# Reordering the opening loads, the first group's loads and the last stores of a fused attention and gated-unit kernel

## The chip, the cores and the metric

The kernel runs on one core of one Trainium2 chip. The metric is device time in microseconds (us), the median over runs; "span" is the time that a profile covers, 1.7 to 1.9 us less than the run's time.

TensorE is called PE in the profile, VectorE DVE, ScalarE ACT, GpSimd POOL, and SyncE, which here only issues DMAs, SP. "PEld" is the loading of weights into TensorE.

## The reference

```python
# x: 1 x 2048 x 640; 32 heads of 192; keys and values: the last W = 512 of 2048 positions
xn = layernorm(x)
s  = attention(xn @ wq, k_cache[last 512], v_cache[last 512]) @ wo      # softmax(q k^T / sqrt(192)) v
h  = sigmoid(xn @ w_gate) * (xn @ w_up)                                # 640 -> 1536
g  = silu(h @ w_down)                                                  # 1536 -> 640
out = x + s * g
```

## The kernel before

The kernel first computes the gate `g` for all 16 row tiles (4 blocks of 512 rows), then the attention in 8 groups of 4 heads, each over the 4 row blocks. Three places matter here.

The opening. Row tile 0 is normalised, transposed on TensorE (`turn_pe`), and used at once, while weights and further tiles still arrive. Two weight loads are issued by ScalarE, all else by SyncE:

```python
def turn_pe(t):
    pT = ...                                             # one PSUM bank
    for c in range(NCD):
        nc.tensor.transpose(pT[:, c, :], ln[t][:, c * P:(c + 1) * P], ident[:])
    nc.scalar.activation(xnT[:, 0, 3:NCD, r], pT[:, 3:NCD, :], AF.Copy)   # two copies out,
    nc.vector.tensor_copy(xnT[:, 0, 0:3, r], pT[:, 0:3, :])               # one after the other

load_f(nc.scalar, wg_sb, wg_r, 0, 2)      # column blocks 0 and 1 of w_gate: rows of 512 bytes, 320 KB
load_f(nc.scalar, wu_sb, wu_r, 0, 2)      # the same of w_up
load_x(0, 1)                              # row tiles, 160 KB each, on SyncE
load_x(1, 1)
load_x(2, 2)
for f0, f1 in ((2, 4), (4, 8), (8, NF)):
    load_f(nc.sync, wg_sb, wg_r, f0, f1)
    load_f(nc.sync, wu_sb, wu_r, f0, f1)
...
piece(0, 0, lambda: normal(1))            # piece(t, f): tile t, column block f, 2 x 5 matmuls
piece(0, 1, first_half(2), 1)             # with turn_pe(1) in front
piece(1, 0, second_half(2))
piece(1, 1)
piece(0, 2, lambda: normal(2))
...                                       # 16 pieces in all, then matmuls over all 512 rows
```

The middle. Further blocks are transposed by DMA from SyncE (`turn_dma`, `xnT<-xn`). Behind the third block's loop GpSimd issues the loads of the first head group, 2.5 MB:

```python
def load_group(g):                        # wq, keys, values: nc.gpsimd.dma_start(...) throughout
...
if b == 2:
    load_group(0)
```

The tail. `u` numbers the units of group and block; `turn_out` transposes the attention output by DMA (`oT<-o_st`) and `project` multiplies by `wo`, gates, adds and stores. In the last unit the transposes come in halves, the stores go to ScalarE's queue, one add runs on GpSimd, and the last row tile is cut in three:

```python
for h, k in enumerate((2, 0, 1, 3)):
    values(u, h, k)
    if h % 2:
        turn_out(u, 3 * (h // 2), 3 * (h // 2) + 3)          # 4 half transposes, twice, on SyncE
for q, k in ((1, 2), (2, 0), (3, 1)):
    project(u - 1, q, k, nc.scalar)
for q, k in ((0, 3), (1, 2), (2, 0)):
    project(u, q, k, nc.scalar, None, nc.gpsimd if q == 2 else None)
project(u, 3, (1, 3, 2), None, ((0, 256), (256, 512), (512, D)))
# in project: r_sb = fin.tile([P, D], BF16, name="row")      # a ring of 4 buffers
```

The softmax here doesn't subtract the row's maximum and nothing guards it: scores larger than these inputs give would overflow.

Of the kernel before, what the change touches and what calls it, by code (L numbers as in the profile page):

```python
# [8 lines left out]
AF = mybir.ActivationFunctionType  # L9
# [6 lines left out]
def kernel(  # L16
# [76 lines left out]
    def load_group(g):  # L93

        d = grp.setdefault(g, {})
        d["wq"] = load2.tile([P, NCD, GW], BF16, name="wq_sb")
        nc.gpsimd.dma_start(d["wq"][:], wq_r[:, :, g * GW:(g + 1) * GW])
        kst = load1.tile([P, 4, KC, DH], BF16, name="k_st")
        kv = slice(Sk - W, Sk)
        nc.gpsimd.dma_start(  # L100
            kst[:].rearrange("p h j d -> p h (j d)"),
            A_k_cache[0, 4 * g:4 * g + 4, kv, :].rearrange("h (p j) d -> p h (j d)", j=KC),
        )
        d["v"] = vbuf[g % 2]
        for h in range(4):
            nc.gpsimd.dma_start(  # L106
                d["v"][:, h, :, 0:DH],
                A_v_cache[0, 4 * g + h, kv, :].rearrange("(p j) d -> p j d", j=KC),
            )
        kp = load1.tile([P, 2, KC, DJ, P], BF16, name="k_perm")  # L110
        for h in range(4):
            nc.gpsimd.tensor_copy(
                kp[:, h // 2, :, :, (h % 2) * H2:(h % 2) * H2 + H2],
                kst[:, h, :, :].rearrange("p c (i j) -> p c j i", j=DJ),
            )
        d["kp"] = kp
# [17 lines left out]
    with ExitStack() as bctx:  # L134
# [11 lines left out]
        def load_x(t, n):  # L146

            x = xpool.tile([P, n, D], BF16, name=f"x_sb{n}", bufs=1 if n == 2 else 2)
            nc.sync.dma_start(x[:], xf[t * P:(t + n) * P, :].rearrange("(q p) d -> p q d", p=P))
            for i in range(n):  # L150
                xt[t + i] = x[:, i, :]
# [5 lines left out]
        load_f(nc.scalar, wg_sb, wg_r, 0, 2)  # L157
        load_f(nc.scalar, wu_sb, wu_r, 0, 2)
        load_x(0, 1)
        load_x(1, 1)  # L160
        load_x(2, 2)
        for f0, f1 in ((2, 4), (4, 8), (8, NF)):
            load_f(nc.sync, wg_sb, wg_r, f0, f1)
            load_f(nc.sync, wu_sb, wu_r, f0, f1)
# [42 lines left out]
        def turn_pe(t):  # L207

            pT = bank[3][:, t % 2, 0:NCD * H2].bitcast(BF16).rearrange("p (c n) -> p c n", c=NCD)
            for c in range(NCD):  # L210
                nc.tensor.transpose(pT[:, c, :], ln[t][:, c * P:(c + 1) * P], ident[:])
            r = slice(t * P, (t + 1) * P)
            nc.scalar.activation(xnT[:, 0, 3:NCD, r], pT[:, 3:NCD, :], AF.Copy)
            nc.vector.tensor_copy(xnT[:, 0, 0:3, r], pT[:, 0:3, :])
# [7 lines left out]
        def gated(b, f, r0, r1, k, between=None):  # L222
            if b not in hT:
                hT[b] = hpool.tile([P, NF, TB], BF16, name="hT")
            for half, w in ((0, wg_sb), (1, wu_sb)):
                for c in range(NCD):
                    nc.tensor.matmul(bank[k][:, half, 0:r1 - r0], lhsT=w[:, c, f * P:(f + 1) * P],  # L227
                                     rhs=xnT[:, b, c, r0:r1], start=(c == 0), stop=(c == NCD - 1))
            sig = bwork.tile([P, TB], BF16, name="sig")
# [31 lines left out]
        dummy(19)  # L261
# [8 lines left out]
        stats_end(1)  # L270
        k = 0

        def piece(t, f, before=None, turn=None):
            nonlocal k
            if turn is not None:
                turn_pe(turn)
            gated(0, f, t * P, (t + 1) * P, k, before)
            k = (k + 1) % 3

        def first_half(t):  # L280
            return lambda: stats_half(t, 0)
# [5 lines left out]
        piece(0, 1, first_half(2), 1)  # L287
        piece(1, 0, second_half(2))
        piece(1, 1)
        piece(0, 2, lambda: normal(2))  # L290
        piece(0, 3, first_half(3))
        piece(1, 2, second_half(3))
        piece(1, 3, None, 2)
        piece(2, 0, lambda: normal(3))
        piece(2, 1)
        piece(2, 2)
        piece(2, 3, None, 3)
# [6 lines left out]
        for b in range(1, NB):  # L304
# [11 lines left out]
            if b == 2:  # L316
                load_group(0)
# [89 lines left out]
    def turn_out(u, c0=0, c1=GC):  # L407
        if u not in oT:
            oT[u] = oT_pool.tile([P, GC, TB], BF16, name="oT")
        for q in range(TQ):  # L410
            nc.sync.dma_start_transpose(oT[u][:, c0:c1, q * P:(q + 1) * P],  # L411
                                        o_st[u][:, q, c0 * P:c1 * P])

    def project(u, q, k, out_eng=None, parts=None, add_eng=None):
# [3 lines left out]
        last = g == NG - 1  # L418
        split = ((0, 512), (512, D))
        if parts is None:  # L420
            for cc in range(GC):
                for d0, d1 in split:
                    nc.tensor.matmul(wide(k)[:, d0:d1], lhsT=oT[u][:, cc, q * P:(q + 1) * P],  # L423
                                     rhs=wo[:, cc, d0:d1], start=(cc == 0), stop=(cc == GC - 1))
            if last:
                o_sb = fin.tile([P, D], F32, name="o_sb", bufs=2)
                r_sb = fin.tile([P, D], BF16, name="row")
                nc.vector.tensor_tensor(o_sb[:], wide(k)[:, 0:D], gate[:, t, :], ALU.mult)  # L428
                (add_eng or nc.vector).tensor_tensor(r_sb[:], o_sb[:], acc[:, t, :], ALU.add)  # L429
                out_eng.dma_start(of[t * P:(t + 1) * P, :], r_sb[:])  # L430
            elif g == 0:
                nc.vector.tensor_copy(acc[:, t, :], wide(k)[:, 0:D])
            else:
                nc.vector.tensor_tensor(acc[:, t, :], wide(k)[:, 0:D], acc[:, t, :], ALU.add)  # L434
        else:

            o_sb = fin.tile([P, D], F32, name="o_sb", bufs=2)
            r_sb = fin.tile([P, D], BF16, name="row")
            for i, (d0, d1) in enumerate(parts):
                ps = wide(k[i])[:, 0:d1 - d0]  # L440
                for cc in range(GC):
                    nc.tensor.matmul(ps, lhsT=oT[u][:, cc, q * P:(q + 1) * P],
                                     rhs=wo[:, cc, d0:d1], start=(cc == 0), stop=(cc == GC - 1))
                nc.vector.tensor_tensor(o_sb[:, d0:d1], ps, gate[:, t, d0:d1], ALU.mult)
                nc.vector.tensor_tensor(r_sb[:, d0:d1], o_sb[:, d0:d1], acc[:, t, d0:d1], ALU.add)  # L445
                eng = (nc.scalar, nc.sync)[i % 2]
                eng.dma_start(of[t * P:(t + 1) * P, d0:d1], r_sb[:, d0:d1])
        if g == NG - 2:
# [5 lines left out]
    for u in range(NU):  # L454
# [8 lines left out]
        if b == 1 and g + 1 < NG:  # L463
            load_group(g + 1)
# [19 lines left out]
    for h, k in enumerate((2, 0, 1, 3)):  # L484
        values(u, h, k)
        if h % 2:
            turn_out(u, 3 * (h // 2), 3 * (h // 2) + 3)
    for q, k in ((1, 2), (2, 0), (3, 1)):
        project(u - 1, q, k, nc.scalar)
    for q, k in ((0, 3), (1, 2), (2, 0)):  # L490
        project(u, q, k, nc.scalar, None, nc.gpsimd if q == 2 else None)
    project(u, 3, (1, 3, 2), None, ((0, 256), (256, 512), (512, D)))
# [30 lines left out]
```

## Time and profile before

| | before |
|---|---|
| time, median (range of its first 3 runs) | 940.91 us (940.86 to 941.36) |
| span of the profile | 939.5 us |
| TensorE busy | 919.6 us (98%) |
| first real matmul / first dense 512-column matmul | 7.12 / 21.19 us |
| last values matmuls begin | 914.38 us |
| last VectorE instruction ends | 936.27 us |

Lines of the profile's page, before: the span; the busy time of each engine, with its share of the span and its instructions; and the chain of work that ended last, by engine.

```profile
span 939.5 us, 18100 instructions
...
PE 919.6 (98%) x7962; PEld 548.1 (58%) x8042; DVE 471.0 (50%) x754; ACT 305.8 (33%) x342; POOL 132.5 (14%) x161
...
PE 95%; DMA 2%; DVE 1%; issue 1%; ACT 0%; SPq 0%; POOL 0%; DVEq 0%
```

TensorE does nearly all of the work and is nearly all of the chain. So its idle time is what can be won. The list of waits of TensorE over the whole span, before; each line reads who waited, on what line, for whom, then the total in us, the number of waits and the longest:

```profile
engine line waited for: us in total, times, longest us
PE bank L227 <- DMA xnT<-xn: 3.4, 1, 3.4
PE bank L423 <- DMA oT<-o_st: 2.2, 2, 1.7
PE bank L227 <- DVE xnT L214: 1.6, 3, 0.7
PE bank L211 <- DVE xn L203: 1.5, 2, 1.3
PE bank L177 <- DVE eps_t L168: 1.2, 1, 1.2
```

These are waits at the edges. The first is one wait in the middle, at 116 us, for the DMA transposes of the last activation block; the second lies in the tail; the third and fourth in the opening (the fifth is the start itself). From 172 to 900 us there is next to none.

Stretches of the opening, before (start and end in us; busy us and instructions of each engine; then the granted TensorE clock, the DMA share and GB/s):

```profile
core 0: us, PE busy (x) PEld busy (x) DVE busy (x) ACT busy (x) POOL busy (x), PEclk, DMA share, GB/s
5.20:8.60 3.40, 1.71 (x20) 1.13 (x18) 1.90 (x7) 1.75 (x4) 0.57 (x1) 1.00 1.16 311
8.60:12.00 3.40, 2.91 (x28) 2.91 (x29) 2.13 (x7) 0.68 (x3) 0.00 (x0) 0.51 1.10 344
```

In the second stretch TensorE is busy, but at half of its clock (0.51): groups of five 128-column matmuls follow each other every 0.53 us there, and every 0.28 us from 12.2 us on. Ahead of it lies a stretch with 1.71 us of work in 3.4.

The transposes of activations (`xnT`), 95 to 125 us, before: the four issues (duration of an issue in ns, first and last start), who made TensorE idle and for how long, and the time from issue to landing:

```profile
L218 SPq DMA_TRANSPOSE xnT<-xn x4: 1200/1202/1202, 102.9 to 110.1; - x4
...
  DMA xnT<-xn: 3.4, 1
...
DMA to landing us min/median/max: 2.6/2.6/9.3
```

Three land in 2.6 us, one in 9.3. In this time GpSimd's 2.5 MB arrive.

The end of the chain of work that ended last, before (start, duration, what):

```profile
924.94 1.27 SPq L411
...
926.26 4.90 DMA oT<-o_st
...
931.21 1.00 PE bank L423 x6
...
932.23 0.04 DVE o_sb L428
...
933.42 1.53 DVE row L445
...
935.98 0.29 DVE row L445
```

SyncE is still issuing transposes at 926.2 us, one of them lands 4.9 us later, TensorE goes on at 931.21, and VectorE closes. Its add of 256 columns at 933.42 us takes 1.53 us while an add of GpSimd's runs (933.14 to 934.68 us); its next one of that size takes 0.42.

### The profile page before, as it was taken

What the parts mean: (1) busy time and instruction counts of PE and PEld (TensorE: products, weight loads), DVE (VectorE), ACT (ScalarE), POOL (GpSimd) and SP (SyncE); (2) the same over time, 40 slices, a digit from 0 to 9 for tenths busy, and PEclk for the clock granted to TensorE, in tenths of its full rate; (3) what the DMA queues carried; (4) which work ended last, traced back from release to release, by engine and by line L of the source; (5) the groups of instructions that cost most, each with busy time, mean ns of one, the idle gap of its engine ahead of it and who ended that gap; (6) DMA issues with size and microseconds to landing.
All of it is one profiled execution on the core that took longest, in us unless ns stands there. A gap on an engine that the chain in (4) does not pass through costs nothing.

```text
span 939.5 us, 18100 instructions
## 1 busy us (share of the span) xinstructions
PE 919.6 (98%) x7962; PEld 548.1 (58%) x8042; DVE 471.0 (50%) x754; ACT 305.8 (33%) x342; POOL 132.5 (14%) x161
## 2 busy tenths in 40 slices
PE   8999999999999999999999999999999999999996
PEld 6445444466666666666666666666666666666664
DVE  5553523355555555555555555555555555555657
ACT  3222212343333333333333333333333333333340
POOL 1000210300020002000200020002000205555000
PEclk9999999999999999999999999999999999999999
DMA  9300330424423343424343433273325343422323
GB/s 310 84 19 11 96 76 1 154 74 81 101 65 76 65 114 68 76 56 123 68 77 56 122 68 77 54 124 68 77 51 127 69 79 70 87 67 58 63 67 86
DMA packets 156767, 76.69 MB, mean 82 GB/s; under 512 B 139024, under 2 KB 150032, under 8 KB 156688
## 3 DMA queue, kind: packets, MB, share of 16 engines
q1 hardware_dynamic: 146288, 42.86, 23.5%
q0 software_dynamic: 7936, 30.94, 11.9%
q10 hardware_dynamic: 2464, 1.74, 0.7%
q8 instruction: 63, 1.03, 0.5%
q14 instruction: 16, 0.13, 0.1%
HBM read 39.45 MB, written 2.62 MB: 45 GB/s over the span
## 4 chain that ended last, share of the span: by engine, by line
PE 95%; DMA 2%; DVE 1%; issue 1%; ACT 0%; SPq 0%; POOL 0%; DVEq 0%
PE bank L381 21%; PE bank L423 21%; PE bank L398 18%; PE bank L363 18%; PE bank L227 10%; PE bank L239 6%; DMA xnT<-xn 1%; PE bank L331 1%; DMA oT<-o_st 1%; DMA x_sb<-in_A_x_dram 0%; DVE row L445 0%; DVE st L185 0%; DVE row L429 0%; DVE o_sb L428 0%; SPq L411 0%
## 5 line engine op out<-in xcount | busy, mean ns | idle before, releaser
L367 ACT ACTIVATE E<-bank 128x1024 bf16<-128x1024 f32 x256 | 257.8, 1023 | 477.5 <-PE bank L363 465.5
L381 PE MATMUL bank<-xnT,wq_sb 64*128 64x512 bf16 x1860 | 231.4, 376 | 0.0
L423 PE MATMUL bank<-wo_sb,oT 128*128 128x512 bf16 (+1 forms) x1461 | 224.0, 296 | 5.5 <-DMA oT<-o_st 2.2
L363 PE MATMUL bank<-qT,kT 64*128 64x512 bf16 x1536 | 202.2, 377 | 0.2 <-DVE o_st L404 0.2
L398 PE MATMUL bank<-vbuf,E 128*128 128x193 bf16 x2048 | 191.0, 247 | 0.0
L398 PEld LDWEIGHTS <-E 128*128 128x128 bf16 x2048 | 167.8, 98 | 24.2 <-issue 13.6
L388 DVE CAST qT<-bank 128x1024 bf16<-128x1024 f32 x93 | 113.9, 1225 | 132.8 <-PE bank L381 132.8
L423 PEld LDWEIGHTS <-oT 128*128 128x128 bf16 x1524 | 120.1, 98 | 78.8 <-DMA oT<-o_st 2.8
L381 PEld LDWEIGHTS <-wq_sb 64*128 64x128 bf16 x1860 | 97.3, 100 | 104.5
L363 PEld LDWEIGHTS <-kT 64*128 64x128 bf16 x1536 | 73.3, 94 | 90.0 <-issue 8.9
L404 DVE TENSOR_TENSOR o_st<-bank,rden 128x768 bf16<-128x768 f32 x128 | 122.6, 958 | 4.6 <-DVE rden L403 0.2
L434 DVE TENSOR_TENSOR acc<-bank,acc 128x640 f32<-128x640 f32 x96 | 79.2, 825 | 43.7 <-PE bank L423 43.7
L227 PE MATMUL bank<-xnT,wg_sb 128*128 128x512 bf16 (+1 forms) x296 | 62.1, 340 | 5.2 <-DMA xnT<-xn 3.4
L227 PE MATMUL bank<-xnT,wu_sb 128*128 128x512 bf16 (+1 forms) x295 | 62.1, 339 | 0.3
L386 DVE COPY seen<-bank 128x2 f32<-128x2 f32 x93 | 14.8, 160 | 94.1 <-PE bank L381 93.9
L233 DVE TENSOR_TENSOR hT<-bank,sig 128x512 bf16<-128x512 f32 (+1 forms) x60 | 35.0, 583 | 51.1 <-ACT sig L230 51.1
L403 DVE RECIPROCAL rden<-bank 128x4 f32<-128x4 f32 x128 | 23.4, 182 | 71.3 <-PE bank L398 71.2
L230 ACT ACTIVATE sig<-bank 128x512 bf16<-128x512 f32 (+1 forms) x60 | 30.7, 512 | 79.7 <-PE bank L227 76.6
L239 PE MATMUL bank<-wd_sb,hT 128*128 128x128 bf16 (+1 forms) x376 | 52.4, 298 | 0.4
L106 POOL DMA_DIRECT2D vbuf<-in_A_v_cache_dram x32 | 23.9, 747 | 183.7 <-PE bank L398 183.7
L227 PEld LDWEIGHTS <-wg_sb 128*128 128x128 bf16 x300 | 27.2, 100 | 31.1 <-issue 5.9
L239 PEld LDWEIGHTS <-hT 128*128 128x128 bf16 x384 | 29.6, 98 | 23.2
(49 smaller groups left out, 264.9 us busy)
## 6 DMA issues: line engine op xcount, KB each, us to landing
wq_sb<-in_A_wq_dram POOLq DMA_DIRECT2D x8, 960.0 KB, 6.8
wo_sb<-in_A_wo_dram POOLq DMA_DIRECT2D x8, 960.0 KB, 7.1
k_st<-in_A_k_cache_dram POOLq DMA_DIRECT2D x8, 768.0 KB, 8.7
vbuf<-in_A_v_cache_dram POOLq DMA_DIRECT2D x32, 192.0 KB, 3.0
row<-in_A_x_dram POOLq DMA_DIRECT2D x16, 160.0 KB, 2.7
oT<-o_st SPq DMA_TRANSPOSE x132, 2.6
x_sb<-in_A_x_dram SPq DMA_DIRECT2D x3, 640.0 KB, 10.8
wd_sb<-in_B_w_down_dram SPq DMA_DIRECT2D x1, 1920.0 KB, 14.0
```

Source lines behind the costliest of these rows:

```text
L227: nc.tensor.matmul(bank[k][:, half, 0:r1 - r0], lhsT=w[:, c, f * P:(f + 1) * P], rhs=xnT[:, b, c, r0:r1], start=(c == 0), stop=(c == NCD - 1))
L230: nc.scalar.activation(sig[:, 0:r1 - r0], bank[k][:, 0, 0:r1 - r0], AF.Sigmoid)
L233: nc.vector.tensor_tensor(hT[b][:, f, r0:r1], bank[k][:, 1, 0:r1 - r0], sig[:, 0:r1 - r0], ALU.mult)
L239: nc.tensor.matmul(wide(k)[:, d0:d1], lhsT=hT[b][:, f, q * P:(q + 1) * P], rhs=wd_sb[:, f, d0:d1], start=(f == 0), stop=(f == NF - 1))
L363: nc.tensor.matmul(bank[k][:, i, :], lhsT=kT[r, pr, j, c * P:(c + 1) * P], rhs=q[r, pr * DJ + j, :], start=(j == 0), stop=(j == DJ - 1))
L367: nc.scalar.activation(E[u, pr][:, c, :, :], bank[k][:], AF.Exp, scale=scale_qk)
L381: nc.tensor.matmul(bank[k][:, half, :], lhsT=wq[r, c, col:col + DJ * (P - 1) + 1:DJ], rhs=xnT[r, b, c, :], start=(c == 0 and not second), ...
L388: nc.vector.tensor_copy(qT[u][:, 2 * m:2 * m + 2, :], bank[k][:])
L398: nc.tensor.matmul(o4[:, q, 0:DH + 1], lhsT=e[:, c, h % 2, q * P:(q + 1) * P], rhs=v[:, h, c, 0:DH + 1], start=(c == 0), stop=(c == KC - 1))
L404: nc.vector.tensor_tensor(o_st[u][:, :, h * DH:(h + 1) * DH], o4[:, :, 0:DH], rden[:].to_broadcast([P, TQ, DH]), ALU.mult)
L423: nc.tensor.matmul(wide(k)[:, d0:d1], lhsT=oT[u][:, cc, q * P:(q + 1) * P], rhs=wo[:, cc, d0:d1], start=(cc == 0), stop=(cc == GC - 1))
L434: nc.vector.tensor_tensor(acc[:, t, :], wide(k)[:, 0:D], acc[:, t, :], ALU.add)
```

## The change

The intent: put the opening loads on one queue in the order in which they are needed; copy each opening transpose out of PSUM with one engine; run four pieces of tile 0 before tile 1 is needed and put the transposes inside a piece; load the first head group behind the transposes on SyncE's own queue; and in the tail transpose whole, with the stores of the last-but-one unit queued behind the transposes. Two small companions are not shown: one more warm-up matmul at the start (20 for 19) and four single-tile buffers for the row tiles of the opening.

```diff
-    def load_group(g):
+    def load_group(g, eng):
-        nc.gpsimd.dma_start(d["wq"][:], wq_r[:, :, g * GW:(g + 1) * GW])
+        eng.dma_start(d["wq"][:], wq_r[:, :, g * GW:(g + 1) * GW])
 ...                                                   (keys and values likewise)
-        load_f(nc.scalar, wg_sb, wg_r, 0, 2)
-        load_f(nc.scalar, wu_sb, wu_r, 0, 2)
         load_x(0, 1)
+        load_f(nc.sync, wg_sb, wg_r, 0, 2)
         load_x(1, 1)
-        load_x(2, 2)
-        for f0, f1 in ((2, 4), (4, 8), (8, NF)):
+        load_f(nc.sync, wu_sb, wu_r, 0, 2)
+        load_x(2, 1)
+        load_f(nc.sync, wg_sb, wg_r, 2, 4)
+        load_f(nc.sync, wu_sb, wu_r, 2, 4)
+        load_x(3, 1)
+        for f0, f1 in ((4, 8), (8, NF)):
 ...
-            nc.scalar.activation(xnT[:, 0, 3:NCD, r], pT[:, 3:NCD, :], AF.Copy)
-            nc.vector.tensor_copy(xnT[:, 0, 0:3, r], pT[:, 0:3, :])
+            if t == 0:
+                nc.vector.tensor_copy(dst, pT)
+            else:
+                nc.scalar.activation(dst, pT, AF.Copy)
 ...                               (gated() gets amid: turn_pe between its gate and its up matmuls)
-        piece(0, 1, first_half(2), 1)
-        piece(1, 0, second_half(2))
-        piece(1, 1)
-        piece(0, 2, lambda: normal(2))
-        piece(0, 3, first_half(3))
-        piece(1, 2, second_half(3))
-        piece(1, 3, None, 2)
+        piece(0, 1)
+        piece(0, 2, second_half(2), 1)
+        piece(0, 3)
+        piece(1, 0, lambda: normal(2))
+        piece(1, 1, lambda: stats_half(3, 0))
+        piece(1, 2, second_half(3), 2)
+        piece(1, 3)
 ...
-                load_group(0)
+                load_group(0, nc.sync)
 ...
     for h, k in enumerate((2, 0, 1, 3)):
         values(u, h, k)
-        if h % 2:
-            turn_out(u, 3 * (h // 2), 3 * (h // 2) + 3)
+    turn_out(u)
     for q, k in ((1, 2), (2, 0), (3, 1)):
-        project(u - 1, q, k, nc.scalar)
+        project(u - 1, q, k, nc.sync)
     for q, k in ((0, 3), (1, 2), (2, 0)):
-        project(u, q, k, nc.scalar, None, nc.gpsimd if q == 2 else None)
-    project(u, 3, (1, 3, 2), None, ((0, 256), (256, 512), (512, D)))
+        project(u, q, k, nc.scalar)
+    project(u, 3, 1, None)                 # one product, two adds and two stores (384 and 256 columns)
```

More of the change, by code (lines that the diff above doesn't have):

```diff
@@ L91 @@
     grp = {}
-    def load_group(g):
+    def load_group(g, eng):
         d = grp.setdefault(g, {})
         d["wq"] = load2.tile([P, NCD, GW], BF16, name="wq_sb")
-        nc.gpsimd.dma_start(d["wq"][:], wq_r[:, :, g * GW:(g + 1) * GW])
+        eng.dma_start(d["wq"][:], wq_r[:, :, g * GW:(g + 1) * GW])
         kst = load1.tile([P, 4, KC, DH], BF16, name="k_st")
         kv = slice(Sk - W, Sk)
-        nc.gpsimd.dma_start(
+        eng.dma_start(
             kst[:].rearrange("p h j d -> p h (j d)"),
@@ L105, in load_group @@
         for h in range(4):
-            nc.gpsimd.dma_start(
+            eng.dma_start(
                 d["v"][:, h, :, 0:DH],
@@ L146, in load_x @@
         def load_x(t, n):
-            x = xpool.tile([P, n, D], BF16, name=f"x_sb{n}", bufs=1 if n == 2 else 2)
+            x = xpool.tile([P, n, D], BF16, name=f"x_sb{n}", bufs=4 if n == 1 else 2)
             nc.sync.dma_start(x[:], xf[t * P:(t + n) * P, :].rearrange("(q p) d -> p q d", p=P))
@@ L211, in turn_pe @@
                 nc.tensor.transpose(pT[:, c, :], ln[t][:, c * P:(c + 1) * P], ident[:])
-            r = slice(t * P, (t + 1) * P)
-            nc.scalar.activation(xnT[:, 0, 3:NCD, r], pT[:, 3:NCD, :], AF.Copy)
-            nc.vector.tensor_copy(xnT[:, 0, 0:3, r], pT[:, 0:3, :])
+            dst = xnT[:, 0, :, t * P:(t + 1) * P]
+            if t == 0:
+                nc.vector.tensor_copy(dst, pT)
+            else:
+                nc.scalar.activation(dst, pT, AF.Copy)
         def turn_dma(t):
@@ L220, with gated @@
         hT = {}
-        def gated(b, f, r0, r1, k, between=None):
+        def gated(b, f, r0, r1, k, between=None, amid=None):
             if b not in hT:
@@ L228, in gated @@
                                      rhs=xnT[:, b, c, r0:r1], start=(c == 0), stop=(c == NCD - 1))
+                if half == 0 and amid is not None:
+                    turn_pe(amid)
             sig = bwork.tile([P, TB], BF16, name="sig")
@@ L258, in norm_piece @@
             return step if i <= TQ else None
-        dummy(19)
+        dummy(20)
         stats_half(0, 0)
@@ L270, with piece @@
         stats_end(1)
+        stats_half(2, 0)
         k = 0
-        def piece(t, f, before=None, turn=None):
+        def piece(t, f, before=None, amid=None):
             nonlocal k
-            if turn is not None:
-                turn_pe(turn)
-            gated(0, f, t * P, (t + 1) * P, k, before)
+            gated(0, f, t * P, (t + 1) * P, k, before, amid)
             k = (k + 1) % 3
-        def first_half(t):
-            return lambda: stats_half(t, 0)
         def second_half(t):
@@ L286 @@
         piece(0, 0, lambda: normal(1))
-        piece(0, 1, first_half(2), 1)
-        piece(1, 0, second_half(2))
-        piece(1, 1)
-        piece(0, 2, lambda: normal(2))
-        piece(0, 3, first_half(3))
-        piece(1, 2, second_half(3))
-        piece(1, 3, None, 2)
+        piece(0, 1)
[5 more added lines that the diff above has]
+        piece(1, 3)
         piece(2, 0, lambda: normal(3))
         piece(2, 1)
-        piece(2, 2)
-        piece(2, 3, None, 3)
+        piece(2, 2, None, 3)
+        piece(2, 3)
         for f in range(4):
@@ L405, in values, with turn_out, project @@
                                 rden[:].to_broadcast([P, TQ, DH]), ALU.mult)
-    def turn_out(u, c0=0, c1=GC):
-        if u not in oT:
-            oT[u] = oT_pool.tile([P, GC, TB], BF16, name="oT")
+    def turn_out(u):
+        oT[u] = oT_pool.tile([P, GC, TB], BF16, name="oT")
         for q in range(TQ):
-            nc.sync.dma_start_transpose(oT[u][:, c0:c1, q * P:(q + 1) * P],
-                                        o_st[u][:, q, c0 * P:c1 * P])
-    def project(u, q, k, out_eng=None, parts=None, add_eng=None):
+            nc.sync.dma_start_transpose(oT[u][:, :, q * P:(q + 1) * P], o_st[u][:, q, :])
+    def project(u, q, k, out_eng):
         g, b = u // NB, u % NB
@@ L417, in project @@
         t = b * TQ + q
-        last = g == NG - 1
-        split = ((0, 512), (512, D))
-        if parts is None:
-            for cc in range(GC):
-                for d0, d1 in split:
-                    nc.tensor.matmul(wide(k)[:, d0:d1], lhsT=oT[u][:, cc, q * P:(q + 1) * P],
-                                     rhs=wo[:, cc, d0:d1], start=(cc == 0), stop=(cc == GC - 1))
-            if last:
-                o_sb = fin.tile([P, D], F32, name="o_sb", bufs=2)
-                r_sb = fin.tile([P, D], BF16, name="row")
-                nc.vector.tensor_tensor(o_sb[:], wide(k)[:, 0:D], gate[:, t, :], ALU.mult)
-                (add_eng or nc.vector).tensor_tensor(r_sb[:], o_sb[:], acc[:, t, :], ALU.add)
-                out_eng.dma_start(of[t * P:(t + 1) * P, :], r_sb[:])
-            elif g == 0:
-                nc.vector.tensor_copy(acc[:, t, :], wide(k)[:, 0:D])
-            else:
-                nc.vector.tensor_tensor(acc[:, t, :], wide(k)[:, 0:D], acc[:, t, :], ALU.add)
-        else:
+        for cc in range(GC):
+            for d0, d1 in ((0, 512), (512, D)):
+                nc.tensor.matmul(wide(k)[:, d0:d1], lhsT=oT[u][:, cc, q * P:(q + 1) * P],
+                                 rhs=wo[:, cc, d0:d1], start=(cc == 0), stop=(cc == GC - 1))
@@ L437, in project @@
+        if g == NG - 1:
             o_sb = fin.tile([P, D], F32, name="o_sb", bufs=2)
             r_sb = fin.tile([P, D], BF16, name="row")
+            nc.vector.tensor_tensor(o_sb[:], wide(k)[:, 0:D], gate[:, t, :], ALU.mult)
+            parts = ((0, D),) if out_eng is not None else ((0, 384), (384, D))
             for i, (d0, d1) in enumerate(parts):
-                ps = wide(k[i])[:, 0:d1 - d0]
-                for cc in range(GC):
-                    nc.tensor.matmul(ps, lhsT=oT[u][:, cc, q * P:(q + 1) * P],
-                                     rhs=wo[:, cc, d0:d1], start=(cc == 0), stop=(cc == GC - 1))
@@ L444, in project @@
-                nc.vector.tensor_tensor(o_sb[:, d0:d1], ps, gate[:, t, d0:d1], ALU.mult)
                 nc.vector.tensor_tensor(r_sb[:, d0:d1], o_sb[:, d0:d1], acc[:, t, d0:d1], ALU.add)
-                eng = (nc.scalar, nc.sync)[i % 2]
+                eng = out_eng or (nc.scalar, nc.sync)[i]
                 eng.dma_start(of[t * P:(t + 1) * P, d0:d1], r_sb[:, d0:d1])
+        elif g == 0:
+            nc.vector.tensor_copy(acc[:, t, :], wide(k)[:, 0:D])
+        else:
+            nc.vector.tensor_tensor(acc[:, t, :], wide(k)[:, 0:D], acc[:, t, :], ALU.add)
@@ L463 @@
         if b == 1 and g + 1 < NG:
-            load_group(g + 1)
+            load_group(g + 1, nc.gpsimd)
             load_wo(g + 1)
```

## The prediction

> **What bounds the kernel.** TensorE. The page's busy table has it busy 919.6 of 939.5 us, and the chain of waits puts 95% of the span on its matmuls. The list of waits shows hardly any from 172 to 900 us. So only three places can give time.
>
> 1. Opening. In the timeline the dense 512-column matmuls start at 21.19 us. The first real matmul starts at 7.12 us; 16 pieces of ten 128-column matmuls (0.56 us each at full rate) and three transposes (0.28 us each) need 9.8 us, but took 14.07. It waits 1.25 us for the second normalised tile, 1.6 for transposed copies. From about 8.8 to 12.2 us the stretches view shows a granted clock of 0.52: 31 matmuls took 3.1 us where full rate gives 1.74. The Trainium skill ("TensorE: Matmul & The Clock Gate", Part 1) says a mostly idle window of about 3.4 us halves the clock; the trace agrees: one halved window of 3.4 us, after a window with 1.7 us of work.
> 2. Middle, at 116 us: TensorE idles 3.35 us for the last transpose of the last activation block. That one took 9.3 us to land, its siblings 2.6; GpSimd's 2.5 MB for the first head group moves beside it (303 GB/s at 116 to 120 us).
> 3. Tail. After the last values (919.9 us) TensorE waits 0.5 and 1.7 us for transposes; the last took 4.9 us to land against a median of 2.5, beside output stores from the other queue. Each transpose, whole or half, costs 1.25 us to issue; there are eight halves. The last matmul ends at 933.84, VectorE at 936.27 (one add took 1.53 us beside GpSimd's), the span at 939.5.
>
> **The change, costed.**
> 1. The first tile is alone at the head of the queue: lands about 2.8 us instead of 3.41. ScalarE loses two issues (1 us). The first transposed copy, 0.62 us on VectorE alone, no longer waits for ScalarE's table load. First real matmul about 6.2. Four pieces of tile 0 run before tile 1 is needed, and transposes sit inside pieces. The opening bytes move at about 340 GB/s as before, so the third piece may wait some 0.5 us for weights and for tile 1's normalisation (about 8.2 us). TensorE does about 2.4 us of work in the window that before had 1.7, so I expect no halved clock (60%). Dense matmuls from about 17.1: gain 4 us; 2.5 if the halved window returns.
> 2. First-group loads go on the transposes' own queue, behind them: the last lands in about 2.6 us, before it is needed. Gain 3.35.
> 3. Four whole transposes from about 921.2 us, issued by 926.3, no stores beside them: landings about 923.7, 925.0, 926.2, 927.5. TensorE runs through to about 931.1. VectorE (seven times 1.68 us from 921.5) then is the limit, ending about 933.3 instead of 936.3. Gain 2.9.
>
> All three are critical, one after another, so they add: 10.2 us. **Predicted 930.8 us, 80% range 928.6 to 933.4.** Faster by over 2% (under 922): 1%; within 2%: 98.5%; slower: 0.5%.
>
> **Right or wrong shows in:** first real matmul near 6.2 us, first 512-column matmul near 17, no clock of 0.5 there; no idle of TensorE before the last activation block and transposes all landing in about 2.6 us; no TensorE wait for transposes in the tail, last VectorE instruction about 3.2 us before the end.
>
> **What would make it wrong:** weights landing later behind the tiles on one queue, and the idle time halving the clock again; VectorE stuck behind the third tile's statistics; a block of loads still slowing the transpose ahead of it; row buffers held up by stores queued behind the transposes.

## The result, and the profile after

The changed kernel takes 932.92 us (median of 4 runs, 932.66 to 933.39) against 941.13 us (4 runs, 940.86 to 942.36) of the kernel before in the same rounds. The ratio is 0.9911, with a 95% interval of 0.9894 to 0.9928: 8.2 us less, within 2%. A ratio here is the mean time of one kernel's fast runs over that of the other's of the same rounds, so not quite the ratio of the medians quoted.

Lines of the profile's page, after:

```profile
span 931.5 us, 18073 instructions
...
PE 917.8 (99%) x7957; PEld 546.1 (59%) x8037; DVE 469.3 (50%) x749; ACT 306.2 (33%) x341; POOL 126.5 (14%) x154
...
PE 97%; DMA 1%; DVE 1%; issue 1%; SPq 0%; DVEq 0%
```

The waits of TensorE, after (line 231 is line 227 of before):

```profile
engine line waited for: us in total, times, longest us
PE bank L231 <- DMA wg_sb<-in_B_w_gate_dram: 1.4, 1, 1.4
PE bank L180 <- DVE eps_t L171: 1.2, 1, 1.2
PE bank L231 <- DMA wu_sb<-in_B_w_up_dram: 0.6, 2, 0.4
PE bank L231 <- DVE xnT L216: 0.3, 1, 0.3
```

The waits for transposes by DMA are gone, in the middle and in the tail. New are waits for weights in the opening: 1.4 us for a gate block (`wg_sb`) and 0.6 us, in two waits, for up blocks (`wu_sb`).

The same stretches of the opening, after:

```profile
5.20:8.60 3.40, 2.26 (x29) 1.69 (x28) 2.85 (x10) 1.41 (x4) 0.57 (x1) 1.00 1.05 293
8.60:12.00 3.40, 2.22 (x37) 2.06 (x38) 1.30 (x6) 1.26 (x3) 0.55 (x1) 1.00 1.10 349
```

The granted clock is 1.00 in both. In the second stretch TensorE is now busy for only 2.22 of 3.4 us: that is the wait for weights. The first 512-column matmul starts at 19.06 us.

The transposes of activations, 95 to 125 us, after:

```profile
L222 SPq DMA_TRANSPOSE xnT<-xn x4: 1200/1200/1201, 100.8 to 108.0; - x4
...
DMA to landing us min/median/max: 2.6/2.6/2.6
```

All four land in 2.6 us, and no idle time is put down to them.

The end of the chain, after, and below it the one wait of VectorE in the tail that is new:

```profile
914.39 1.32 PE bank L420 x9
...
919.86 0.84 DVE row L429
...
920.73 3.84 DMA out_dram<-row
...
924.67 0.34 DVE row L429
...
927.85 0.56 DVE row L429
```

```profile
DVE row L429 <- DMA out_dram<-row: 1.6, 1, 1.6
```

TensorE is no longer in this last part. SyncE issues the first of the queued stores at 920.73 us, behind the transposes; that store lands 3.84 us later; and VectorE, which wanted its row buffer, goes on at 924.67.

Where the 8.0 us between the two spans come from, by four marks that both traces have:

| stretch | before | after | gain | predicted |
|---|---|---|---|---|
| start to first 512-column matmul | 21.19 | 19.06 | 2.13 | 4.0 |
| from there to the first query matmul (171.61 / 165.97 us) | 150.42 | 146.91 | 3.51 | 3.35 |
| from there to the last values matmuls (914.38 / 908.56 us) | 742.77 | 742.59 | 0.18 | 0 |
| from there to the end | 25.12 | 22.94 | 2.18 | 2.9 |
| span | 939.5 | 931.5 | 8.0 | 10.2 |

All three gains are there, and two are smaller than predicted. The experiments ask whether the parts add, why each acts, and where the missing 2.2 us went.

### The profile page after: what moved, and what is told of

Read it like the earlier page. It is cut to its first block, busy times and chain, and to the rows that moved or that the text cites. A ratio compares the mean times of both kernels' runs of the same rounds, so it can differ in the third digit from the quotient of the medians.

```text
span 931.5 us, 18073 instructions
## 1 busy us (share of the span) xinstructions
PE 917.8 (99%) x7957; PEld 546.1 (59%) x8037; DVE 469.3 (50%) x749; ACT 306.2 (33%) x341; POOL 126.5 (14%) x154
## 4 chain that ended last, share of the span: by engine, by line
PE 97%; DMA 1%; DVE 1%; issue 1%; SPq 0%; DVEq 0%
PE bank L383 22%; PE bank L420 21%; PE bank L400 19%; PE bank L365 18%; PE bank L231 11%; PE bank L245 6%; DMA wu_sb<-in_B_w_up_dram 1%; PE bank L333 1%; DVE o_sb L425 0%; DMA out_dram<-row 0%; DVE row L429 0%; SPq L149 0%; SPq L154 0%; PE bank L213 0%; DVEq L505 0%
## 5 line engine op out<-in xcount | busy, mean ns | idle before, releaser
L420 PE MATMUL bank<-wo_sb,oT 128*128 128x128 bf16 (+1 forms) x1473 | 225.2, 296 | 3.3
L106 POOL DMA_DIRECT2D vbuf<-in_A_v_cache_dram x28 | 20.9, 747 | 184.9 <-PE bank L400 184.9
```

The lines of the kernel that those rows point to most:

```text
L420: nc.tensor.matmul(wide(k)[:, d0:d1], lhsT=oT[u][:, cc, q * P:(q + 1) * P], rhs=wo[:, cc, d0:d1], start=(cc == 0), stop=(cc == GC - 1))
```

## The experiments

There were twelve runs, all correct. e1 to e4 ran on one chip, e5 to e8 on a second, and e9 to e12 on a third. The changed kernel measured 932.92 us, and 933.11 us beside e6 to e8; it did not run beside e9 to e12. So its times are compared with some care, for differences of about 1 us and more.

### Each part alone: e1, e2, e3

e1 is the kernel before with the opening part alone (the loads' order and queue, the single-engine copies, the order of pieces). e2 has the first group's loads on SyncE alone. e3 has the tail part alone. Their edits are the parts of the diff above; of e2 this is nearly all:

```diff
-                load_group(0)
+                load_group(0, nc.sync)
```

Expected of e1: 

> The kernel before with the opening part of the change alone. If the three parts act in separate places and add, this one gains what the opening shows in the two traces: dense 512-column matmuls at about 19.1 us instead of 21.2, so 2.1 us (about 939.0 us against 941.1), with the old stall of 3.4 us at the last activation block and the old tail still there. Rival: the parts depend on each other (a shifted opening makes the middle stall larger or smaller), and then the gain is below 1 or above 3 us. It also tells whether the halved clock between 9 and 12 us is gone whatever else runs: theory says yes.

Expected of e2: 

> The kernel before with the first head group loaded by SyncE alone. Theory: the loads now stand behind the four transposes of the last activation block, each lands in 2.6 us and TensorE's wait of 3.35 us before that block is gone: gain 3.3 to 3.5 us (about 937.7 us). Opening and tail as before. Rival, that the wait was only put down to the transpose and another release would end as late: gain under 1 us, with another wait at the same place.

Expected of e3: 

> The kernel before with the tail part alone (whole transposes, stores of the last-but-one block on SyncE behind them, add on VectorE). Theory: TensorE no longer waits in the tail, VectorE waits about 1.6 us for a row buffer whose store stood behind the transposes; gain about 2.2 us (938.9 us). Rival: the tail gains only together with the others: under 1 us.

Measured, with the kernel before at 941.31 us (11 runs):

| | time, us | ratio (95% interval) | what its profile shows |
|---|---|---|---|
| e1, opening | 939.61 | 0.9979 (0.9966 to 0.9992) | dense matmuls at 18.67 us, no halved clock there; the 3.4 us wait in the middle and 1.9 us of waits in the tail stay |
| e2, group | 937.06 | 0.9953 (0.9941 to 0.9964) | all four transposes land in 2.6 us, the wait in the middle is gone; opening and tail as before |
| e3, tail | 939.28 | 0.9979 (0.9965 to 0.9994) | no TensorE wait in the tail; VectorE waits 1.44 us for a row buffer; the 3.5 us wait in the middle stays |

The product of the three ratios is 0.9911, the ratio that the whole change gave. The parts add, as the prediction had it, though the three intervals together leave some 2 us either way; each profile also shows its own part's wait gone and the others' in place. The rivals (they depend on each other) find no support. Which of the tail's four edits (whole transposes, the stores' queue, the add, the split of the last tile) brings its gain is not parted here. e2 gains 4.4 us, more than the 3.4 us of the wait that it removes; the interval reaches from 3.4 to 5.6 us, and e3's profile shows one way in which the wait can cost more than itself. In that run the old wait in the middle, which ended at 118.8 us, was followed by a stretch at half clock:

```profile
119.20:122.00 2.80, 2.80 (x8) 0.99 (x7) 0.00 (x0) 0.00 (x0) 2.80 (x4) 0.50 0.32 82
```

In the profiles of before and of e1 the same wait was not followed by one. The changes of the clock give the edges of windows of 3.41 us: in e3 nearly the whole wait fell into one window (115.48 to 118.90 us, with 0.08 us of TensorE work), in before and e1 it lay across two (1.80 and 1.67, and 1.84 and 1.54 us of work). So this cost comes in some executions only, and that it explains e2's surplus is likely but not shown.

The opening of before has such a lottery too. e3 has the old opening untouched, and in its profile there is no halved stretch there: its dense matmuls start at 20.20 us, against 21.19 and 21.39 in the profiles of before and e2, where the clock was halved. About 1 us of the opening's gain is thus the avoided halved stretch. The Trainium skill ("TensorE: Matmul & The Clock Gate", Part 1) says that the deciding window is free-running, does not start with the kernel, and makes the cold stretch run-variable; these profiles agree: counted back from a change of the clock in each trace, an edge falls at 5.25 us in before, at 6.01 in e2 and at 6.26 in e3. The window ahead of the halved one held 1.66 us of TensorE work in before, 1.62 in e2 and 1.63 in e10. The busy time of a window alone gives no border, though: 1.81 us (e3, 6.26 to 9.67 us), 1.72 us (the changed kernel, 8.08 to 11.50 us) and the 1.54 us in e1's middle were not followed by a halved window.

### Why the middle wait is gone: e4 and e8

Two explanations fit e2: in one queue the loads stand behind the transposes; or GpSimd's software descriptors were the disturbance, and SyncE's hardware descriptors are not.

```diff
e4:
-                load_group(0, nc.sync)
+                load_group(0, nc.scalar)
```

Expected of e4: 

> The changed kernel, with the first head group loaded by ScalarE at the same point of the program: also hardware descriptors, but a queue other than the transposes'. Theory (order in one queue is what protects the transposes): the last transpose of the last activation block again takes well over 5 us to land and TensorE idles 2 to 4 us for it, so 2 to 4 us longer than the changed kernel. Rival (GpSimd's software descriptors were the disturbance): transposes land in 2.6 us, no idle, time as the changed kernel within 0.5 us.

Measured: 932.84 us, all transposes landed in 2.6 us, no wait. That looks like the rival, but the trace shows that the experiment missed: ScalarE works in program order and issued the loads only at 113.27 us, behind its last sigmoid of the block, while the last transpose had been issued at 107.1. They never met. So e8 issues the same loads from ScalarE earlier:

```diff
e8:
                 gated(b, f, 0, TB, k, ...)
                 k = (k + 1) % 4
-            if b == 2:
-                load_group(0, nc.sync)
+                if b == 2 and f == 8:
+                    load_group(0, nc.scalar)
```

Expected of e8: 

> The changed kernel with the first head group loaded from ScalarE right behind the sigmoid of the ninth column block, about 0.3 us before the last transpose of that activation block is issued: hardware descriptors, another queue, the same moment as GpSimd had. The earlier run on ScalarE issued 6 us too late to collide and tells nothing. Theory (any bulk load that is in flight from another queue slows the transpose): it lands in over 5 us, TensorE idles 2 us or more, time 2 to 4 us over the changed kernel. Rival (only GpSimd's software descriptors do that): it lands in about 2.6 us and the time is as the changed kernel within 0.7 us.

Measured: 934.26 us, against 933.11 us of the changed kernel run once more beside it (e5), so 1.15 us longer. The transposes of activations, 95 to 125 us, in e8:

```profile
L222 SPq DMA_TRANSPOSE xnT<-xn x4: 1200/1200/1201, 100.5 to 107.7; - x4
...
  DMA xnT<-xn: 0.9, 1
...
DMA to landing us min/median/max: 2.6/2.6/7.0
```

The loads were issued at 107.44 us, the last transpose at 107.7, and it landed in 7.0 us. So hardware descriptors on another queue disturb a transpose too: the rival falls. The size was overestimated: TensorE waited 0.9 us and not 2 or more. Whether GpSimd's descriptors add something of their own (9.3 against 7.0 us) was not tested. What protects the transpose is that the bulk does not move at the same time, either because it stands behind it in one queue (e2, the change) or because it comes later (e4). The Trainium skill ("DMA: Bandwidth & Descriptors", Queues, rings and completion order) says that each DMA engine goes round-robin between the queues that have work for it; a transpose that shares the engines with 2.5 MB of another queue is then slowed throughout, which agrees with 7.0 and 9.3 us against 2.6.

### The tail's new wait: e5, e6, e7

e5 is the changed kernel, unedited, as the measure for its neighbours. e6 gives the row ring six buffers. e7 puts the three stores of the last-but-one unit back on ScalarE's queue.

```diff
e6:
-            r_sb = fin.tile([P, D], BF16, name="row")
+            r_sb = fin.tile([P, D], BF16, name="row", bufs=6)     (also x_sb, of the same ring)
e7:
     for q, k in ((1, 2), (2, 0), (3, 1)):
-        project(u - 1, q, k, nc.sync)
+        project(u - 1, q, k, nc.scalar)
```

Expected of e5: 

> The changed kernel once more, unedited, as the measure for the runs beside it on the same chip. Expected 932 to 934 us, dense matmuls of the opening from 18 to 19.2 us (the landing of the second pair of weight blocks differs by some tenths of a us between executions), and the 1.6 us wait of VectorE for a row buffer in the tail.

Expected of e6: 

> The changed kernel with six row buffers instead of four. Theory (the stores queued behind the transposes hold the row buffers, VectorE waits 1.58 us, and the tail ends with VectorE): the wait is gone, VectorE's last instruction comes 1.2 to 1.6 us sooner after the last values matmul, time 1.0 to 1.6 us below the changed kernel. Rival (VectorE would have waited for TensorE or for the two o_sb buffers anyway): under 0.4 us.

Expected of e7: 

> The changed kernel with the three stores of the last-but-one block back on ScalarE's queue, beside the transposes. Theory (stores on another queue slow a transpose, as the 4.9 us landing before the change): at least one of the last four transposes lands in over 3.5 us; TensorE waits up to 1 us for it; but VectorE's wait for row buffers is gone, so the time is within 1 us of the changed kernel, either way. Rival (the slow landing came from eight half transposes alone): all land in 2.6 us, and the time is 1 to 1.6 us below the changed kernel.

Measured:

| | time, us | values matmuls begin to end of span | row-buffer wait |
|---|---|---|---|
| e5, as changed | 933.11 (932.80 to 933.42) | 23.03 us | 1.66 us |
| e6, six buffers | 931.40 (931.31 to 931.52) | 21.44 us | none |
| e7, stores on ScalarE | 931.15 (931.06 to 931.92) | 21.51 us | none |

All waits of VectorE from 910 us on in e6:

```profile
DVE rden L405 <- PE bank L400: 0.4, 2, 0.2
DVE o_sb L425 <- PE bank L420: 0.4, 1, 0.4
```

The wait for a store's landing is gone, and with it 1.6 us of the tail, as the theory for e6 said. In time e6 is 1.7 us and e7 2.0 us below e5, on the same chip, a little more than expected. e7 does as much as e6 without the buffers. There the transposes of the output landed, from 900 us on, in

```profile
DMA to landing us min/median/max: 2.5/2.6/3.2
```

so the stores beside them cost at most 0.6 us for one transpose and no wait of TensorE. The theory that I had put forward for e7, that stores on another queue slow the transposes to over 3.5 us, is wrong, and with it a part of the prediction: the stores were not the main cause of the 4.9 us landing before. What the packets of before show instead: at 929.25 us one 16 KB packet of the queue that fetches instructions occupies one DMA engine for 0.92 us. From 929 to 931.2 us that queue has this one packet:

```profile
q8 instruction: 1, 0.02, 2.6%
```

Just behind it, seventeen packets of a store take 1.2 to 1.3 us each, where such packets take about 0.06 us otherwise, and the last 24 packets of the late transpose come one at a time, taking 26 to 58 ns each, where they usually take 18. The same picture stands in the profiles of e1 and e2 (fetches of 1.40 and 1.20 us, store packets of 0.8 to 1.1 us, landings of 4.6 and 4.5 us). In the changed kernel a fetch of the same kind comes at 921.6 us, when the last packet of the last transpose has just moved (921.5 us). So the four whole transposes are done before the fetch, eight halves were not.

The rest of the traces bears this out, and without stores. Over the fourteen profiles, 875 transposes of the output had neither a fetch nor a load or store beside them: they landed in 2.57 us in the median, none over 3.21. Another 227 had no load or store beside them either, but a 16 KB fetch ran somewhere between 1.3 and 2.5 us after their issue: 4.1 us in the median, 5.3 at most. So such late landings come with a fetch alone, with no store near. No run moved the fetch: this rests on coincidences, but on many.

### Where the opening's missing 1.9 us are: e9 and e10

In the changed opening TensorE waits 0.26, 1.37 and 0.37 us for weights, together 2.0 us. The prediction had allowed some 0.5 us for this, so 1.5 of the 1.96 us that the opening lacks against it (dense matmuls at 19.06 us against 17.1) are here. The second pair of weight blocks (column blocks 2 and 3) is used at 9.41 and 10.51 us, just after it lands; in the kernel before it landed at 8.3 and 9.5 (issued at 2.14 and 2.65, 6.2 and 6.8 us to landing). It comes later although less stands ahead of it: 1760 KB must arrive for the last of these blocks, and 1920 KB in the kernel before. The first of the waits on this pair:

```profile
9.41 0.45 PE L231 MATMUL bank<-xnT,wg_sb 128*128 128x128 bf16 x5 [1.37 <-DMA wg_sb<-in_B_w_gate_dram]
```

Stretch 4 to 6 us of before, then of after:

```profile
4.00:6.00 2.00, 1.78 (x13) 1.07 (x12) 1.54 (x5) 1.38 (x2) 0.00 (x0) 1.00 1.13 337
```

```profile
4.00:6.00 2.00, 1.94 (x16) 1.33 (x15) 1.47 (x5) 1.71 (x3) 0.00 (x0) 1.00 0.97 277
```

One queue moves 277 GB/s where two moved 337. In the six other profiles with the changed loads on one queue this stretch reads 216 to 283, in e2 and e3 with two queues 325 and 328. From 4 to 8 us it is 271 to 293 in the seven with one queue, and 316 to 324 in the three with two. Packets of the weight loads are one row of two column blocks, 512 bytes. When the 2,560 of them end, counted in us from the first data packet:

```
                         2400th   last
before, two queues        6.47    7.09
e2,     two queues        6.34    6.97
after,  one queue         6.66    8.13
e4,     one queue         6.51    7.18
e7,     one queue         6.63    7.32
e5,     one queue         6.39    7.67
e6,     one queue         6.61    7.75
```

In the changed kernel's profile the last 28 packets come one at a time, 23 to 31 ns apart, as from a single engine that is behind, and a load has landed only when its last packet has. This end differs between executions, and the start of the dense matmuls goes with it, not with the rate from 4 to 6 us: e4 and e7 have the lowest rates (216 and 236 GB/s) but the earliest ends, and their dense matmuls start at 18.13 and 18.28 us. The changed kernel's own profile is the latest of the seven; in the six others TensorE waits 0.9 to 1.7 us for weights, not 2.0, and the dense matmuls start at 18.13 to 18.77 us. e9 puts the first pair of weight loads back on ScalarE's queue. e10 keeps one queue and makes the rows longer.

```diff
e9:
-        load_f(nc.sync, wg_sb, wg_r, 0, 2)
+        load_f(nc.scalar, wg_sb, wg_r, 0, 2)
-        load_f(nc.sync, wu_sb, wu_r, 0, 2)
+        load_f(nc.scalar, wu_sb, wu_r, 0, 2)
e10:
         load_x(0, 1)
-        load_f(nc.sync, wg_sb, wg_r, 0, 2)
+        load_f(nc.sync, wg_sb, wg_r, 0, 4)        # rows of 1024 bytes, 640 KB
         load_x(1, 1)
-        load_f(nc.sync, wu_sb, wu_r, 0, 2)
+        load_f(nc.sync, wu_sb, wu_r, 0, 4)
         load_x(2, 1)
-        load_f(nc.sync, wg_sb, wg_r, 2, 4)
-        load_f(nc.sync, wu_sb, wu_r, 2, 4)
         load_x(3, 1)
```

Expected of e9: 

> The changed kernel with the first two weight loads (column blocks 0 and 1 of both matrices) back on ScalarE's queue, the order on SyncE's queue otherwise as changed. Question: why the second pair of weight blocks lands at 9 to 10.5 us in the changed opening, a microsecond later than before although 160 KB less stand ahead of it. Theory (one queue of 512-byte packets moves less per us than two queues side by side, about 280 against 320 GB/s from 2 to 8 us, and one straggling engine holds the last packets): the second pair lands by 8.3 and 9.4 us as before, the dense matmuls start 0.3 to 0.9 us sooner than in the changed kernel's runs (18.1 to 19.1 us), although the first tile lands some 0.3 us later. Rival (issue order and issue time alone decide): the second pair moves by no more than what two issues fewer on SyncE give, 0.9 us, at an unchanged rate of about 280 GB/s.

Expected of e10: 

> The changed kernel with each matrix's first four column blocks in one load, so rows of 1024 bytes instead of two loads with rows of 512, same bytes, one queue. Theory (packet size limits the rate): about 340 GB/s from 3 us on, the set of four tiles and four blocks of both matrices is in by 9 us instead of 10.5 to 11; the first up matmul waits until about 7.8 us, after that TensorE runs without gaps and the dense matmuls start at about 17.4 us (changed kernel 18.1 to 19.1), time 0.8 to 1.5 us below the changed kernel. Rival (rate does not depend on packet size): the last block lands at 9.5 us or later, and the first up matmul waits for all of it, so dense matmuls start at 19.5 us or later and the time is worse by 0.5 us or more.

Measured. e9 takes 932.02 us (931.79 to 932.21), e10 932.97 us (932.63 to 934.27). Stretch 4 to 6 us of e9, then of e10:

```profile
4.00:6.00 2.00, 2.00 (x15) 1.48 (x14) 1.36 (x5) 1.64 (x3) 0.00 (x0) 1.00 1.14 323
```

```profile
4.00:6.00 2.00, 2.00 (x16) 1.41 (x14) 0.88 (x4) 1.64 (x3) 0.00 (x0) 1.00 1.09 382
```

The start of the dense matmuls in e9:

```profile
17.52 1.24 PE L231 MATMUL bank<-xnT,wg_sb 128*128 128x512 bf16 x5
```

In e9 the rate is back at 323 GB/s, the last short packet ends 6.76 us after the first, the second pair of weights is used at 8.08 and 9.19 us, and the dense matmuls start at 17.52 us, 0.6 us or more sooner than in any profile with the single queue (18.13 to 19.06). The time is about 1 us below the changed kernel's, measured in another call. The first tile lost little: its statistics start at 3.16 us against 3.10, the first real matmul at 6.57 us against 6.33. So the single queue was what held the weights. The second pair is also issued 1.1 us sooner in e9 (2.13 instead of 3.26 us), and lands 1.3 us sooner. The issue is an unlikely cause: when the changed kernel issues the pair, at 3.26 us, only 278 of the 1120 KB issued ahead of it have moved, so it stands in a queue anyway. Those 1120 KB are the same in both kernels. Whether the rate, the late last packets or the order in which two queues are served counts most is not parted.

e10 shows that the size of the packets limits the rate: the same queue moves 382 GB/s with 1024-byte rows (367 from 4 to 8 us, against 271 to 293). But it is not faster. Tile 1 now stands behind 640 KB, and VectorE, in its fixed order, waits for its statistics before it can copy the first transpose:

```profile
6.57 0.49 DVE L186 BATCH_NORM_STATS2 st<-x_sb 128x6 f32<-128x320 bf16 x1 [1.26 <-DMA x_sb<-in_A_x_dram]
```

The first real matmul starts at 7.50 us instead of 6.33, the first up matmul at 8.46, TensorE had too little work in between, and the clock was halved. Stretch 10 to 12 us of e10:

```profile
10.00:12.00 2.00, 2.00 (x21) 2.00 (x20) 1.17 (x5) 1.06 (x3) 0.55 (x1) 0.50 1.10 351
```

The dense matmuls start at 19.82 us. The rival's number for this came true (19.5 or later), but not for its reason.

### Both corrections together: e11 and e12

e11 is the changed kernel with e7's stores and e9's two queues. e12 is e11 with 1024-byte rows, the gate block on ScalarE's queue and the up block on SyncE's behind tiles 0 and 1.

```diff
e12 against e11:
         load_x(0, 1)
-        load_f(nc.scalar, wg_sb, wg_r, 0, 2)
+        load_f(nc.scalar, wg_sb, wg_r, 0, 4)
         load_x(1, 1)
-        load_f(nc.scalar, wu_sb, wu_r, 0, 2)
+        load_f(nc.sync, wu_sb, wu_r, 0, 4)
         load_x(2, 1)
-        load_f(nc.sync, wg_sb, wg_r, 2, 4)
-        load_f(nc.sync, wu_sb, wu_r, 2, 4)
         load_x(3, 1)
```

Expected of e11: 

> Two corrections together: the changed kernel with the first two weight loads on ScalarE's queue (as e9) and the three stores of the last-but-one block on ScalarE's queue (as e7). Dense matmuls at about 17.5 us (changed kernel 18.1 to 19.1) and no wait of VectorE for a row buffer. The two act in separate places, so the gains should add: about 1.0 and 1.9 us, 930.1 us, that is 2.7 to 3.1 us below the changed kernel. Rival: the stores or loads on ScalarE's queue cost what they gain, 931 us or more.

Expected of e12: 

> As e11, but the first four blocks of the gate weights in one load of 1024-byte rows on ScalarE's queue and those of the up weights in one such load on SyncE's, behind tiles 0 and 1, ahead of tiles 2 and 3. Theory (packet size sets the rate and only what stands ahead of tile 1 spoiled e10): about 350 GB/s from 3 us, tile 1 by 5 us, first gate matmul at about 6.6 us, the up weights by 7.6 us, no halved clock, dense matmuls at 16.8 to 17.3 us, 0.2 to 0.7 us below e11. Rival: the larger block holds the first matmul or the first up matmul beyond 8 us and dense matmuls start at 18 us or later.

Measured, with the kernel before at 942.19 us (8 runs): e11 930.57 us (930.46 to 930.67), ratio 0.9877 (0.9860 to 0.9893); e12 931.32 us (931.28 to 931.50), ratio 0.9886. e11 beats both kernels, by 2.4 us the changed one (932.92 us), a little less than the 2.7 us expected at the least. They were run at other times. By their ratios to the kernel before (0.9877 against 0.9911) it is 3.2 us, so the gains add within what these runs can tell. Its dense matmuls start at 17.57 us. All waits of TensorE that its profile lists:

```profile
PE bank L180 <- DVE eps_t L171: 1.2, 1, 1.2
PE bank L213 <- DVE xn L206: 0.3, 1, 0.3
PE bank L231 <- DVE xnT L216: 0.2, 1, 0.2
```

No wait for a load or a transpose by DMA is left. e12 is 0.75 us slower than e11, so my theory for it fails: its rate was high (372 GB/s from 4 to 6 us) and its clock full, but tile 1's statistics waited until 6.10 us, and the first up matmul waited for its larger block until 8.01 us; dense matmuls start at 18.05 us. In the opening the moment at which the first block is complete counts for more than the rate.

## Why the prediction was right or wrong

The time was right: 932.92 us lies in the range of 928.6 to 933.4, near its upper end, and the change stayed within 2%. The mechanism of the gain was right in the opening and in the middle; in the tail the gain came, but one reason given for the old loss did not hold. e1 to e3 show that the three parts add. Two terms of the sum were too large.

- Opening, "gain 4 us": 2.13 us. The first real matmul came at 6.33 us (predicted 6.2), tile 1 was normalised by about 8.3 us (8.2), and the clock was not halved. The failing term is "the third piece may wait some 0.5 us for weights", which rested on "the opening bytes move at about 340 GB/s as before". TensorE waited 2.0 us for weights (0.9 to 1.7 us in the other profiles of this opening): on one queue, the stretch with packets of 512 bytes moved at 271 to 293 GB/s from 4 to 8 us, and the last of them ended up to 1 us late. The 340 GB/s was read over the whole opening, in which most bytes come in longer rows. e9 takes the weights' wait down to about 0.4 us and starts the dense matmuls at 17.5 us; from its first real matmul to there it takes 10.95 us, where the prediction had 10.9.
- Clock. "No halved clock (60%)" held in every profile with the changed order of pieces, but for e10, where tile 1 came late. I had taken the halved stretch for a fixed cost of the kernel before; e3 shows that it meets only some of its executions, at about 1 us. That it held was also luck: in the window from 8.08 to 11.50 us the changed kernel's TensorE worked only 1.72 us, while waiting for weights, and in before the clock was halved after a window with 1.66. The prediction looked only at the window ahead of that, which it put at 2.4 us.
- Middle, "gain 3.35": 3.51 us. Right, with the stated mechanism; e8 shows that bulk on another queue at that moment slows a transpose, whoever issues it.
- Tail, "gain 2.9": 2.18 us. TensorE ran through as predicted. VectorE's last instruction ended 20.19 us after the values matmuls began, where the prediction had 18.9. The failing term is a wait that the prediction named among its risks, "row buffers held up by stores queued behind the transposes", and gave no size: 1.58 us. e6 and e7 remove it, and then VectorE ends 18.7 us after that mark.
- Tail, the reason given for the slow transpose before, "beside output stores from the other queue": not confirmed. With such stores beside whole transposes the slowest landed in 3.2 us (e7), while instruction fetches with no store beside them go with landings of 4.1 us in the median.

## What to carry to other kernels

Putting loads behind a latency-critical transfer on the same queue protects it, but everything that is queued behind it also holds its buffers longer: count the ring's buffers up to the moment at which the last store lands. A transfer rate read over a whole phase does not hold for its first few microseconds when those packets are shorter or on fewer queues; read it from the stretch where the wait is. Before an experiment with a moved issue is believed, look in its trace whether the issue really came at the moment meant: e4 did not.

## What the Trainium skill lacked or had wrong

- "DMA: Bandwidth & Descriptors", Issuing engines are not separate DMA queues, says that starting DMAs on several engines only saves the sequencer's issue time, and its Rules for kernel authors say that spreading DMAs over engines does not help bandwidth. Here two hardware queues moved 312 to 324 GB/s and one 271 to 293 in the same stretch of the opening (4 to 8 us), with packets of 512 and 1280 bytes; with rows of 1024 bytes one queue reached 367. For short packets a second queue did help.
- The same page explains why small descriptors are slow and works it out for 256 bytes. Here 512-byte packets went at about 30 ns each and 1024-byte ones at about 50, so the stretch with 512-byte rows ran at a fifth to a quarter less on one queue (271 to 293 against 367 GB/s).
- No page gives how long an instruction fetch holds a DMA engine, or what it does to a transfer beside it. The traces show one 16 KB packet about every 14 us, 0.9 to 1.8 us long on one engine (one of 2.1); a transpose with one beside it, and no load or store, landed in 4.1 us in the median instead of 2.57.
- No page gives the landing time of a DMA transpose beside bulk loads: 2.6 us alone, 7.0 us beside 2.5 MB issued by ScalarE, 9.3 us beside the same issued by GpSimd.
- "TensorE: Matmul & The Clock Gate", Part 1, gives a busy or idle window of about 3.4 us and no border between them. Here windows with 1.62 to 1.66 us of TensorE work in the opening were followed by a halved one, but one with 1.72 was not, nor one with 1.54 us of longer matmuls in e1's middle.
